# Pair loads, weight chunks, x loads and the last stacks in one chain of issue, x loads from slot 141, all of x split by GpSimd: attention with a softplus MoE on one core

## The chip, the core and the metric

The kernel runs on one core of a Trainium2 chip. The metric is device time in microseconds of one execution. The core has TensorE (PE, with its weight loads as PEld), VectorE (DVE), ScalarE (ACT), GpSimd (POOL) and SyncE (SP); each takes its own list of instructions in order, and sixteen DMA engines move data. SyncE and ScalarE issue the DMAs of this kernel.

## What is computed

Attention over 4 batches, 8 heads, 576 positions and 64 columns a head, with rotary embedding of q and k, and an MoE feed-forward with softplus on its result, all in 32-bit floats:

```
q_rot, k_rot = (rotate(q), rotate(k))
scores = scale * np.matmul(q_rot, k_rot.transpose(0, 1, 3, 2))
scores = scores - np.max(scores, axis=-1, keepdims=True)
attn = np.exp(scores)
attn = attn / (np.sum(attn, axis=-1, keepdims=True) + 1e-09)
return np.matmul(attn, v).astype(np.float32)
...
x = np.ascontiguousarray(attn_out.transpose(0, 2, 1, 3)).reshape(B * S, H * D)
...
h = x @ w_in
g = np.maximum(h, 0.0) + np.log1p(np.exp(-np.abs(h)))
return (g @ w_out).astype(np.float32)
```

x is 2304 x 512, w_in 512 x 2048, w_out 2048 x 512.

## The kernel before, in words

**Precision.** TensorE works on a reduced 32-bit type, so each operand is held as a rounded high part and a low part (the rest), and a product is three matmuls. Splitting an operand is a rounding and a subtraction.

**Attention: slots.** The 32 heads have five blocks of 128 positions each, which gives 160 slots (`NSLOT`); the loop at line 470 runs `NSLOT + LAG + PVD` = 172 times. In slot s, `p1` makes the scores of block s with keys (line 352), and VectorE takes each row's maximum (line 354). Nine slots later (`LAG`), `p2` makes the scores again, transposed and with the maxima taken off (line 389), ScalarE takes the exponential twice (395, 396), and VectorE the low part (403). Three slots on, `pv_mm` multiplies with v (line 421). When a head is through, `evac` copies its sum out and writes it to `xd` and the row sums to `xs` in device memory (lines 429 to 434); after each batch the sums come back as `rc`, `recip` inverts them on VectorE and writes `rd` (line 445).

**The shift row.** In slot 5h GpSimd rounds the five maxima of the last head (`shift1`, tile `shl`), in slot 5h + 1 TensorE transposes them (`shift2`, line 372), ScalarE casts the result (374) and itself issues the small DMA `qs<-shr` that puts it into two rows of q (`shift3`, line 378). `p2` reads it three slots later.

**Loads.** q and k come by pairs of heads: `load_pair` reads two raw tiles of 576 KB (line 287), `rope_steps` turns them, mostly on GpSimd (line 300) one step a slot, and `stack(h)` copies a head's parts with four DMAs into `qs` and `ks` (lines 331 to 334). A pair's first stack is emitted at slot 10p - 4 for use at slot 10p, the second at 10p for use at 10p + 5. All these DMAs are issued by SyncE.

**Weights.** Each w chunk is 128 x 512 in 64 bits, 512 KB (line 105), and is turned into high and low 32-bit parts by `conv_w` on ScalarE and VectorE, one step per call of a hook. f = 0 is converted at the start; `late` holds the others, begun at slot 138 (`WP`). The chunks of f = 1 have tiles of their own (`wr`), the others share three buffers (`wraw`).

**x.** Its first two batches are brought back while attention still runs: `load_xb` reads for each of eight chunks (two batches, four column blocks) the rows of `xd` (288 KB) and twice the inverse sums from `rd`, spread over 64 partitions (144 KB each). `split_xb` multiplies, rounds (both GpSimd) and subtracts. The subtractions of the second batch's first two chunks are VectorE's (`low_xb`, line 189, slots 161 and 163). `tail(s)`, called at the end of each slot, asks for one load a slot from slot 110 (`XL`) and for one step of a split, sometimes two, from slot 146 (`XS`).

**MoE.** 96 units of 384 rows by 128 columns of h: `emit_h` (line 200, tile hp) and two units later `emit_o` (line 236, tiles oa and ob). The first unit reads x of batch 0 alone, the second also batch 1. The first two are placed in the last slots of attention.

**What sets the order.** Instructions that go through `pin` keep the order in which the program emits them. Others (`free`, or none) are placed by a scheduler on their engine's list, sometimes far ahead of where they were emitted. Each DMA signals one of eight completion counters, taken in turn in the scheduled order, SyncE's and ScalarE's together, and a DMA is issued only when the one before it on the same counter has landed.

## Time and profile before

| | us |
|---|---|
| median of three timed runs | 765.46 (762.35 to 766.77) |
| the profiled execution | 767.87 |
| its span | 766.0 |
| TensorE busy, of the span | 723.5 (94%) |
| VectorE busy | 501.5 (65%) |
| ScalarE busy | 383.7 (50%) |
| GpSimd busy | 307.9 (40%) |

Attention takes the first 357 us or so, the MoE the rest. The timeline of an engine lists its instructions by start, with the length, the source line, what is written from what, and in brackets the idle time ahead with what ended it. A DMA's line (SPq, ACTq) is the time of its issue alone: the data lands later. The row of the maxima on VectorE (line 354) stands once in each slot, so that its starts show the pace.

### The profile page before, as it was taken

How to read it: one execution, taken by the hardware profiler on the slowest of the kernel's cores; microseconds unless marked ns; L12 is line 12 of the kernel's file. 1: busy time of each engine (PE TensorE's matmuls, PEld its weight loads, DVE VectorE, ACT ScalarE, POOL GpSimd, SP SyncE). 2: the span in 40 equal slices, each digit the busy share in tenths (PEclk: the TensorE clock that was granted, in tenths of full speed). 3: DMA queues.
4: the chain of work that ended last, by engine and by line, in shares of the span. 5: the costliest groups of instructions: out<-in, count | busy, mean ns of one | idle time of the engine just before them, and what ended most of it. 6: DMA issues, size and time to landing. Idle time of an engine off the chain costs nothing.

```text
span 766.0 us, 11808 instructions
## 1 busy us (share of the span) xinstructions
PE 723.5 (94%) x4288; PEld 674.9 (88%) x4288; DVE 501.5 (65%) x790; ACT 383.7 (50%) x718; POOL 307.9 (40%) x370
## 2 busy tenths in 40 slices
PE   5579999979998999998999999999999999999997
PEld 5469999978998998997889999998999989899996
DVE  7668888857786787886788888864453444444343
ACT  2157777656775776776566556532222222222221
POOL 6249999958887888891000000083040000000000
PEclk9579999999999999999999999999999999999999
DMA  8967888887877789510233333353010001001001
GB/s 261 261 146 193 210 213 213 219 217 203 213 197 204 207 229 213 133 26 9 92 110 110 112 110 111 97 159 110 1 62 1 1 1 42 1 1 42 0 1 42
DMA packets 46507, 91.41 MB, mean 119 GB/s; under 512 B 6800, under 2 KB 15312, under 8 KB 46448
## 3 DMA queue, kind: packets, MB, share of 16 engines
q1 hardware_dynamic: 43472, 85.77, 41.4%
q10 hardware_dynamic: 2976, 4.88, 1.7%
q8 instruction: 34, 0.56, 0.3%
q14 instruction: 25, 0.20, 0.1%
HBM read 51.00 MB, written 9.58 MB: 79 GB/s over the span
## 4 chain that ended last, share of the span: by engine, by line
PE 60%; DVE 3%; ACT 1%; issue 1%; DMA 1%; POOL 0%; DVEq 0%; ACTq 0%; POOLq 0%; SPq 0%
PE hp L200 25%; PE oa L236 12%; PE ob L236 12%; PE pv L421 4%; PE sp L389 3%; PE sp L352 3%; DVE wc L132 1%; DVE wc L129 1%; DMA ks<-raw 1%; DVE e L210 0%; DVE m L215 0%; DVE wl L137 0%; DVE wc L125 0%; ACT e L212 0%; DVE g L220 0%
## 5 line engine op out<-in xcount | busy, mean ns | idle before, releaser
L200 PE MATMUL hp<-x,wh 128*128 128x384 f32 x768 | 196.3, 336 | 0.0
L354 DVE TENSOR_REDUCE mx<-sp 128x1 f32<-128x576 f32 x160 | 121.0, 756 | 74.8 <-PE sp L352 51.7
L200 PEld LDWEIGHTS hp<-x,wh 128*128 128x128 f32 x768 | 140.7, 188 | 8.6 <-ACT wh L135 0.5
L212 ACT ACTIVATE e<-e 128x384 f32<-128x384 f32 x96 | 50.4, 525 | 186.8 <-DVE e L210 182.1
L352 PE MATMUL sp<-ks,qs 128*128 128x288 f32 x640 | 119.1, 311 | 23.2 <-DMA ks<-raw 17.5
L395 ACT ACTIVATE ph<-sp 128x576 fp32r<-128x576 f32 x160 | 103.8, 649 | 57.3 <-PE sp L389 57.1
L200 PE MATMUL hp<-x,wl 128*128 128x384 f32 x384 | 129.6, 337 | 0.6 <-DVE wl L137 0.5
L352 PEld LDWEIGHTS sp<-ks,qs 128*128 128x128 f32 x640 | 97.2, 197 | 28.8 <-issue 19.3
L389 PE MATMUL sp<-qs,ks 128*128 128x288 f32 x640 | 115.0, 302 | 6.0 <-DMA qs<-shr 4.9
L421 PE MATMUL pv<-ph,vs 128*64 128x288 f32 (+1 forms) x640 | 112.6, 299 | 4.4 <-DVE xt L429 3.4
L396 ACT ACTIVATE sp<-sp 128x576 f32<-128x576 f32 x160 | 102.8, 643 | 0.0
L389 PEld LDWEIGHTS sp<-qs,ks 128*128 128x128 f32 x640 | 94.7, 192 | 8.2 <-DMA qs<-shr 5.4
L210 DVE TENSOR_SCALAR e<-hp 128x384 int32<-128x384 int32 x96 | 53.3, 555 | 73.8 <-PE hp L200 73.4
L403 DVE TENSOR_TENSOR pl<-sp,ph 128x576 fp32r<-128x576 f32 x128 | 96.6, 755 | 6.5 <-ACT sp L396 5.1
L236 PE MATMUL oa<-wh,g 128*128 128x512 f32 x288 | 97.7, 393 | 0.0
L236 PE MATMUL ob<-wh,g 128*128 128x512 f32 x288 | 97.3, 393 | 0.0
L421 PEld LDWEIGHTS pv<-ph,vs 128*64 128x64 f32 (+1 forms) x640 | 88.2, 164 | 5.2 <-ACT ph L395 4.8
L300 POOL TENSOR_TENSOR raw<-raw,tab 128x576 f32<-128x576 f32 x58 | 82.5, 1442 | 8.8 <-DMA raw<-qk 8.8
L220 DVE TENSOR_TENSOR g<-m,g 128x384 fp32r<-128x384 f32 x96 | 56.1, 584 | 44.7 <-ACT g L217 44.7
L215 DVE SCALAR_TENSOR_TENSOR m<-hp,e 128x384 f32<-128x384 f32 x96 | 53.5, 557 | 48.6 <-ACT e L212 48.5
L300 POOL TENSOR_TENSOR raw<-raw 128x576 f32<-128x576 f32 (+1 forms) x56 | 80.8, 1443 | 5.2 <-ACT raw L294 3.0
L217 ACT CAST g<-m 128x384 fp32r<-128x384 f32 x96 | 49.1, 512 | 60.0 <-DVE m L215 57.8
(73 smaller groups left out, 875.8 us busy)
## 6 DMA issues: line engine op xcount, KB each, us to landing
raw<-qk SPq DMA_DIRECT2D x32, 576.0 KB
wraw<-w SPq DMA_DIRECT2D x30, 512.0 KB
ks<-raw SPq DMA_DIRECT2D x32, 320.0 KB
qs<-raw SPq DMA_DIRECT2D x32, 288.0 KB
ks<-raw SPq DMA_DIRECT2D x32, 160.0 KB
vf<-v SPq DMA_DIRECT2D x32, 160.0 KB
qs<-raw SPq DMA_DIRECT2D x32, 144.0 KB
xd<-xt SPq DMA_DIRECT2D x32, 144.0 KB
```

The lines of the kernel that those rows point to most:

```text
L200: pin(nc.tensor.matmul(out=hp, lhsT=a[f][:, c * 128:(c + 1) * 128], rhs=piece(j, c)[:, b, :], start=(i == 0), stop=(i == 11),))
L215: pin(nc.vector.scalar_tensor_tensor(out=m, in0=hp, scalar=0.0, in1=e, op0=ALU.max, op1=ALU.add))
L220: pin(nc.vector.tensor_tensor(out=g[:, 1, :], in0=m, in1=g[:, 0, :].bitcast(F32), op=ALU.subtract))
L236: pin(nc.tensor.matmul(out=po, lhsT=g[:, s, t * 128:(t + 1) * 128], rhs=b[f][:, 512:1024], start=(first and i == 0), stop=(last and i == 2),))
L300: pin((nc.vector if e == "V" else nc.gpsimd).tensor_tensor(out=out, in0=in0, in1=in1, op=op))
L352: pin(nc.tensor.matmul(out=sp[:, j, :HS], lhsT=q[:, i, cq], rhs=k[:, 0, ck], start=(i == 0), stop=(i == 1)))
L354: pin(nc.vector.tensor_reduce(out=mx_t[h][:, c:c + 1], in_=sp[:, :, :HS], axis=AX.XY, op=ALU.max, negate=True))
L389: pin(nc.tensor.matmul(out=sp[:, i, :HS], lhsT=k[:, j, ck], rhs=q[:, j, hs], start=(j == 0), stop=(j == 1)))
L395: pin(nc.scalar.activation(out=ph, in_=sp, func=AF.Exp, scale=D ** -0.5))
L396: pin(nc.scalar.activation(out=sp, in_=sp, func=AF.Exp, scale=D ** -0.5))
L403: pin(nc.vector.tensor_tensor(out=pl, in0=sp[:, :, :HS], in1=ph.bitcast(F32), op=ALU.subtract))
L421: pin(nc.tensor.matmul(out=pv[rows, i, :HS], lhsT=lhs, rhs=rhs[:, i, :], start=(c == 0 and j == 0), stop=(c == 4 and j == len(terms) - 1)))
```

## The change

`chain` makes each DMA that goes through it follow the one that went through before, on SyncE's list. Through it go the weight chunks from f = 1 on, the pair loads from the third pair on, the x loads, and the stacks of the last four heads. `XL` goes from 110 to 141, with two x loads a slot after slot 150. All three steps of each split are GpSimd's; `low_xb` and its two places are gone, and the buffer for the products has two tiles instead of four.

```diff
-XL = 110
+XL = 141
...
+    order = []
+
+    def chain(ins):
+        if order:
+            tc.add_manual_dep(ins.ins, order[-1].ins.name,
+                              mybir.DependencyInfo(mybir.DependencyClass.NoSync, mybir.DependencyReason.DATA))
+        order[:] = [ins]
+        return ins
...
-            (pin if n + f < 2 else free)(nc.sync.dma_start(out=raw.bitcast(w.dtype), in_=w[f, :, i * m:(i + 1) * m]))
+            (pin if f == 0 else chain)(nc.sync.dma_start(out=raw.bitcast(w.dtype), in_=w[f, :, i * m:(i + 1) * m]))
...
-        yield nc.sync.dma_start(out=t[:, 0, :], in_=xd[b, c * 128:(c + 1) * 128, :])
+        yield chain(nc.sync.dma_start(out=t[:, 0, :], in_=xd[b, c * 128:(c + 1) * 128, :]))
...
-            yield nc.sync.dma_start(out=t[i * D:(i + 1) * D, 1, :], in_=src)
+            yield chain(nc.sync.dma_start(out=t[i * D:(i + 1) * D, 1, :], in_=src))
...
-        if e is not None:
-            yield pin(e.tensor_tensor(out=t[:, 1, :], in0=x, in1=t[:, 0, :].bitcast(F32), op=ALU.subtract))
...
+        yield pin(nc.gpsimd.tensor_tensor(out=t[:, 1, :], in0=x, in1=t[:, 0, :].bitcast(F32), op=ALU.subtract))
...
-    def low_xb(b, c):
-        t = half_x(b, c)
-        pin(nc.vector.tensor_tensor(out=t[:, 1, :], in0=xraw[b, c], in1=t[:, 0, :].bitcast(F32), op=ALU.subtract))
...
-                (pin if p < 2 else free)(nc.sync.dma_start(out=r[:, :, :S].bitcast(F32), in_=qk[p, i]))
+                (pin if p < 2 else chain)(nc.sync.dma_start(out=r[:, :, :S].bitcast(F32), in_=qk[p, i]))
...
+            keep = chain if h >= 28 else free
+            keep(nc.sync.dma_start(out=q[64:128, 0, :S], in_=qhl[o, 0, :S]))
...
-        mp["xm"] = pool(es, "xm", 4, "right")
+        mp["xm"] = pool(es, "xm", 2, "right")
...
-                next(loads, None)
+                for _ in range(2 if s > NSLOT - 10 else 1):
+                    next(loads, None)
...
-            if s in lows:
-                low_xb(1, lows[s])
...
-        lows = {NSLOT + 1: 0, NSLOT + 3: 1}
-        splits = (x for i in range(8) for x in split_xb(*divmod(i, 4), None if 4 <= i < 6 else nc.gpsimd))
+        splits = (x for i in range(8) for x in split_xb(*divmod(i, 4)))
```

The lists of TensorE and ScalarE are the same in both kernels; VectorE's lacks the two subtractions, and GpSimd's has them. SyncE's differs above all at three places. In the names, qs_120 to qs_123 and ks_116 to ks_119 are the four stack buffers (head modulo 4), x_72 to x_75 the four column blocks of x.

SyncE in the first slots, before: the pair loads (raw with the tile's number), the weight chunks (wraw) and the stacks of heads 2 and 3 (buffers 2 and 3 of qs and ks).

```order
L331 DMA qs2_122<-raw_205 64x576
L332 DMA qs2_122<-raw_205 64x2x576
L331 DMA qs3_123<-raw_205 64x576
L332 DMA qs3_123<-raw_205 64x2x576
L287 DMA raw_350<-qk 128x2x576
L105 DMA wraw_4660<-w 128x512
L287 DMA raw_462<-qk 128x2x576
L333 DMA ks2_118<-raw_251 64x2x640
L333 DMA ks3_119<-raw_251 64x2x640
L334 DMA ks2_118<-raw_251 64x640
L334 DMA ks3_119<-raw_251 64x640
L105 DMA wraw_4665<-w 128x512
```

And now:

```order
L334 DMA qs2_122<-raw_205 64x576
L335 DMA qs2_122<-raw_205 64x2x576
L289 DMA raw_350<-qk 128x2x576
L334 DMA qs3_123<-raw_205 64x576
L335 DMA qs3_123<-raw_205 64x2x576
L336 DMA ks2_118<-raw_251 64x2x640
L336 DMA ks3_119<-raw_251 64x2x640
L337 DMA ks2_118<-raw_251 64x640
L337 DMA ks3_119<-raw_251 64x640
L289 DMA raw_462<-qk 128x2x576
L289 DMA raw_575<-qk 128x2x576
L320 DMA vf0_124<-v 128x320
```

The two weight chunks are gone from here; of the pair loads raw_350 moved ahead of head 3's q, and raw_462 from ahead of the four ks loads to behind them.

SyncE around slots 62 to 70, before: rd is the first batch's inverse sums, and the stacks are those of heads 14 and 15.

```order
L332 DMA qs_122<-raw 64x2x576
L445 DMA rd<-rc 128x36
L318 DMA vf_125<-v 128x320
L161 DMA x_72<-rd 64x576 x2
L161 DMA x_73<-rd 64x576 x2
L433 DMA xd<-xt 64x576
L434 DMA xs<-xt 1x576
L333 DMA ks_118<-raw 64x2x640
L334 DMA ks_118<-raw 64x640
L331 DMA qs_123<-raw 64x576
```

And now:

```order
L335 DMA qs_122<-raw 64x2x576
L448 DMA rd<-rc 128x36
L320 DMA vf_125<-v 128x320
L336 DMA ks_118<-raw 64x2x640
L436 DMA xd<-xt 64x576
L437 DMA xs<-xt 1x576
L337 DMA ks_118<-raw 64x640
L334 DMA qs_123<-raw 64x576
```

The loads of x from rd, which stood between vf and the ks loads, are gone. The same holds 40 slots later, for the second batch.

SyncE around slots 130 to 150, before: wr are the chunks of f = 1, raw is half of the last pair, qs_120 and ks_116 are head 28's.

```order
L287 DMA raw<-qk 128x2x576
L105 DMA wr<-w 128x512 x2
L433 DMA xd<-xt 64x576
L434 DMA xs<-xt 1x576
L331 DMA qs_120<-raw 64x576
L332 DMA qs_120<-raw 64x2x576
L318 DMA vf_125<-v 128x320
L438 DMA rc<-xs 128x36
```

And now, where wr and that half pair stand, with the end of head 28's stack (ks_116) and head 29's (qs_121, ks_117):

```order
L337 DMA ks_116<-raw 64x640
L289 DMA raw<-qk 128x2x576
L113 DMA wr<-w 128x512 x2
L334 DMA qs_121<-raw 64x576
L335 DMA qs_121<-raw 64x2x576
L336 DMA ks_117<-raw 64x2x640
L337 DMA ks_117<-raw 64x640
L320 DMA vf_124<-v 128x320
L166 DMA x_72<-xd 128x576
L169 DMA x_72<-rd 64x576
```

The chunks wr moved from ahead of head 28's stack to behind it, and rc no longer stands behind them. Some rows further on head 30's k (ks_118) and head 31's q (qs_123) are reached; there the list was

```order
L333 DMA ks_118<-raw 64x2x640
L433 DMA xd<-xt 64x576
L434 DMA xs<-xt 1x576
L334 DMA ks_118<-raw 64x640
L331 DMA qs_123<-raw 64x576
L332 DMA qs_123<-raw 64x2x576
```

and is now

```order
L336 DMA ks_118<-raw 64x2x640
L436 DMA xd<-xt 64x576
L437 DMA xs<-xt 1x576
L337 DMA ks_118<-raw 64x640
L169 DMA x_73<-rd 64x576
L166 DMA x_74<-xd 128x576
L169 DMA x_74<-rd 64x576 x2
L334 DMA qs_123<-raw 64x576
```

with the second chunk's last x load (x_73) and the third's behind head 30's k. On GpSimd, each of the eight splits now has its subtraction; the two that were VectorE's stand right behind their roundings.

## Rows read from the trace of the kernel before

**Rows 1.** Timeline of VectorE: the maxima of slots 21, 66, 72, 109, 113, 146

```profile
67.62 0.76 DVE L354 TENSOR_REDUCE mx<-sp 128x1 f32<-128x576 f32 x1 [0.23 <-PE sp L352]
...
150.15 0.76 DVE L354 TENSOR_REDUCE mx<-sp 128x1 f32<-128x576 f32 x1 [0.22 <-PE sp L352]
...
167.87 0.76 DVE L354 TENSOR_REDUCE mx<-sp 128x1 f32<-128x576 f32 x1 [0.42 <-PE sp L352]
...
238.88 0.76 DVE L354 TENSOR_REDUCE mx<-sp 128x1 f32<-128x576 f32 x1 [0.30 <-PE sp L352]
...
250.41 0.76 DVE L354 TENSOR_REDUCE mx<-sp 128x1 f32<-128x576 f32 x1 [0.40 <-PE sp L352]
...
314.22 0.76 DVE L354 TENSOR_REDUCE mx<-sp 128x1 f32<-128x576 f32 x1 [0.22 <-PE sp L352]
```

**Rows 2.** Timeline of SyncE, slots 67 to 69

```profile
153.19 2.72 SPq L161 DMA_DIRECT2D x<-rd  x4
...
157.18 0.64 SPq L333 DMA_DIRECT2D ks<-raw  x1
```

**Rows 3.** Timeline of TensorE, slot 70

```profile
161.98 1.25 PE L352 MATMUL sp<-ks,qs 128*128 128x288 f32 x4 [3.18 <-DMA ks<-raw]
```

**Rows 4.** Timeline of ScalarE, slot 66: the cast and its load

```profile
149.56 0.26 ACT L374 CAST shr<-sp 10x128 fp32r<-10x128 f32 x1
...
153.03 0.62 ACTq L378 DMA_DIRECT2D qs<-shr  x1
```

**Rows 5.** Timeline of TensorE from the start to 52 us

```profile
23.13 5.87 PE L352 MATMUL sp<-ks,qs 128*128 128x288 f32 x20 [9.40 <-DMA ks<-raw]
...
42.61 1.09 PE L389 MATMUL sp<-qs,ks 128*128 128x288 f32 x3 [4.67 <-DMA qs<-shr]
...
46.70 0.76 PE L352 MATMUL sp<-ks,qs 128*128 128x288 f32 x4 [1.08 <-DMA ks<-raw]
```

**Rows 6.** Timeline of SyncE from the start to 52 us

```profile
3.36 1.66 SPq L105 DMA_DIRECT2D wraw<-w  x3
...
18.32 1.12 SPq L334 DMA_DIRECT2D ks<-raw  x1
```

**Rows 7.** The page, part 2: what the DMA engines moved, in 40 slices

```profile
GB/s 261 261 146 193 210 213 213 219 217 203 213 197 204 207 229 213 133 26 9 92 110 110 112 110 111 97 159 110 1 62 1 1 1 42 1 1 42 0 1 42
```

**Rows 8.** An x load of the MoE alone: its issue on SyncE, its reader on GpSimd

```profile
486.46 1.11 SPq L172 DMA_DIRECT2D wraw<-rd  x2
...
490.87 1.18 POOL L176 TENSOR_TENSOR wraw<-wraw 128x384 f32<-128x384 f32 x1 [134.39 <-DMA wraw<-rd]
```

**Rows 9.** Timeline of ScalarE, slot 6: issue of the first shift row

```profile
35.61 1.24 ACTq L378 DMA_DIRECT2D qs<-shr  x1
```

**Rows 10.** Timeline of SyncE, slots 132 to 137

```profile
285.53 1.08 SPq L105 DMA_DIRECT2D wr<-w  x2
...
295.57 0.33 SPq L438 DMA_DIRECT2D rc<-xs  x1
```

**Rows 11.** Timeline of GpSimd, slots 147 to 163

```profile
317.18 1.47 POOL L176 TENSOR_TENSOR xm<-x 128x576 f32<-128x576 f32 x1
...
320.85 0.21 POOL L297 TENSOR_SCALAR shl<-mx 128x5 fp32r<-128x5 f32 x1
...
344.52 1.44 POOL L179 TENSOR_TENSOR x<-xm,x 128x576 fp32r<-128x576 f32 x1
```

**Rows 12.** Timeline of SyncE, slot 147: the end of head 30's stack of k

```profile
315.70 0.85 SPq L334 DMA_DIRECT2D ks<-raw  x1
```

**Rows 13.** Timeline of TensorE, slot 151: the shift matmul

```profile
322.55 0.22 PE L372 MATMUL sp<-identr,shl 128*10 128x128 f32 x1
```

**Rows 14.** End of attention: VectorE, and TensorE behind it

```profile
347.06 1.26 DVE L189 TENSOR_TENSOR x<-xm,x 128x576 fp32r<-128x576 f32 x1
...
351.78 0.77 PE L421 MATMUL pv<-ph,vs 128*128 128x288 f32 x4 [3.42 <-DVE xt L429]
```

**Rows 15.** The chain that ended last, in order of time

```profile
359.87 2.10 PE hp L200 x12
```

More of the change, by code (lines that the diff above doesn't have):

```diff
@@ L173, in load_x, with split, split_xb @@
         xraw[j, c] = raw, rc
-    def split(x, raw, rc, t, e):
+    def split(x, raw, rc, t):
         yield pin(nc.gpsimd.tensor_tensor(out=x, in0=raw, in1=rc, op=ALU.mult))
         yield pin(nc.gpsimd.tensor_scalar(out=t[:, 0, :], in0=x, scalar1=1.0, scalar2=0.0, op0=ALU.mult, op1=ALU.add))
-        if e is not None:
-            yield pin(e.tensor_tensor(out=t[:, 1, :], in0=x, in1=t[:, 0, :].bitcast(F32), op=ALU.subtract))
-    def split_xb(b, c, e):
+        yield pin(nc.gpsimd.tensor_tensor(out=t[:, 1, :], in0=x, in1=t[:, 0, :].bitcast(F32), op=ALU.subtract))
+    def split_xb(b, c):
         t = half_x(b, c)
         x = mp["xm"].tile([128, S], F32, tag="xm", name="xm")
-        xraw[b, c] = x
-        return split(x, t[:, 0, :].bitcast(F32), t[:, 1, :].bitcast(F32), t, e)
-    def low_xb(b, c):
-        t = half_x(b, c)
-        pin(nc.vector.tensor_tensor(out=t[:, 1, :], in0=xraw[b, c], in1=t[:, 0, :].bitcast(F32), op=ALU.subtract))
+        return split(x, t[:, 0, :].bitcast(F32), t[:, 1, :].bitcast(F32), t)
     def split_x(j, c):
         raw, rc = xraw.pop((j, c))
-        return split(raw, raw, rc, piece(j, c), nc.gpsimd)
+        return split(raw, raw, rc, piece(j, c))
     def emit_h(j, f):
@@ L330, in stack @@
             qhl, khl = hl_t[p, 0].bitcast(F32), hl_t[p, 1].bitcast(F32)
-            nc.sync.dma_start(out=q[64:128, 0, :S], in_=qhl[o, 0, :S])
-            nc.sync.dma_start(out=q[0:64, :, :S], in_=qhl[o, :, :S])
-            nc.sync.dma_start(out=k[0:64], in_=khl[o, 0:1, :].to_broadcast([64, 2, SP]))
-            nc.sync.dma_start(out=k[64:128, 0, :], in_=khl[o, 1, :])
+            keep = chain if h >= 28 else free
+            keep(nc.sync.dma_start(out=q[64:128, 0, :S], in_=qhl[o, 0, :S]))
+            keep(nc.sync.dma_start(out=q[0:64, :, :S], in_=qhl[o, :, :S]))
+            keep(nc.sync.dma_start(out=k[0:64], in_=khl[o, 0:1, :].to_broadcast([64, 2, SP])))
+            keep(nc.sync.dma_start(out=k[64:128, 0, :], in_=khl[o, 1, :]))
         mx_t, sh_t, ps2, p_t, pv_t, rc_t = {}, {}, {}, {}, {}, {}
```

## Prediction

> **What bounds the kernel now.** I read the profile in four steps: the chain of waits and the window table for the stages, the timeline of VectorE for the pace, the timelines of SyncE and TensorE where the pace breaks, and the timeline of GpSimd where the change puts work. From about 390 us the chain is TensorE alone, matmul behind matmul, to the end; the change touches nothing there. So the gain or loss lies in the attention stage before it.
>
> The stage runs in slots, and VectorE's row maximum (line 354) stands once in each, so its starts are a ruler. From slot 21 to slot 66 they go from 67.62 to 150.15 us: 82.53 us in 45 slots, 1.834 us a slot, with no break [rows 1]. From slot 66 to 146 the ruler goes to 314.22: 164.07 us, where 80 slots at that pace are 146.7. **17.4 us are lost between 150 and 314 us.** They are not spread: slots 66 to 72 take 17.72 instead of 11.0 (6.7 lost), 72 to 109 take 71.01 instead of 67.9 (3.1), 109 to 113 take 11.53 instead of 7.3 (4.2), 113 to 146 take 63.81 instead of 60.5 (3.3) [rows 1].
>
> The first and largest shows what ends last. At 153.19 SyncE issues four loads x<-rd (2.72 us); only after them, at 157.18, the ks load of head 14 [rows 2], and TensorE waits 3.18 us for it, until 161.98 [rows 3]. The x loads of slots 110 and later had been moved this far ahead, and SyncE takes its list in order. There is a second path: each DMA in the built program signals one of eight counters in turn and is issued only when the eighth before it has landed. The extra loads push the shift row's load, issued by ScalarE, onto a counter whose last user is late: it stands at 153.03, where the cast that it needs began at 149.56 and takes a quarter of a microsecond [rows 4], and ScalarE's exponentials stand behind it. The 4.2 us at slot 110 are the same four loads for the next batch, and the 3.1 us after slot 72 are mostly GpSimd's rope work, late by what it lost at 68 to 70.
>
> The head of the kernel is the other place. TensorE starts slot 0 at 23.13 after 9.40 us of waiting for ks, waits 4.67 us at 42.61 for the first shift row, and 1.08 us at 46.70 for the third head's ks [rows 5].
>
> **The change, part by part.**
>
> *x loads from slot 141.* All 24 leave the stretch from 73 to 250 us. No order of SyncE between slots 16 and 130 holds anything new. Of the 17.4 us I leave 1.0 for the two reciprocals on VectorE (slots 102 and 142), work that stays. Ends: the whole 16.5, or only the two clusters that directly have x<-rd in front of ks, 6.7 + 4.2 = 10.9. I take 16.4, since the rest follows the clusters on GpSimd's queue or comes from the weight chunks (next). **-16.4.**
>
> *Weight chunks kept late.* Before, five raw chunks of 512 KB are read in the first 40 us, where two are needed: one too many in the issue at 3.36 [rows 6], and the two that the order shows further on. The DMA engines move 261 GB/s there [rows 7], so each is 2.0 us of transfer. The order now has two, and puts a raw load (576 KB, 2.2 us) behind ks of head 2 that stood ahead of it. First wait: ks is issued at 18.32 for 1.12 us [rows 6] and lands at 23.13. A load into SBUF that stood alone landed 3.3 us behind its issue (487.57 to 490.87) [rows 8], which would be 22.7; so between 0.4 and 2.0 us, I take 0.9. Second wait: the shift row is issued 35.61 to 36.85 [rows 9] and lands at 42.6, 5.7 us later; with the queue short of two chunks and one raw load, 3.3 us, so 39.3 with the 0.9: 3.3 earlier. The third wait, 1.08, then falls away, as ks has 3 us less ahead of it. 0.9 + 2.5 + 1.1 = 4.5; ends 0.4 (only the first floor) and 6.5 (all transfers). **-4.5.**
>
> *Weight chunks of f = 1 at slot 138.* Before, they are issued at 285.53, and SyncE's next wait on their counter ends at 295.57 [rows 10], ten microseconds later, with ks of slot 140 behind it; that is most of the 3.3 us lost from 113 to 146, counted above. Now they stand behind the last pair load and ahead of head 29's stack, in slot 138. With the old loss at slot 140 taken out, slot 138 begins near 297 in the old time (314.22 less 8 slots, less 2.4 lost between), and the issue follows at some 298. About 0.7 MB less is queued ahead of them, 2.7 us at the 261 GB/s, so the second lands near 305 to 307. The eighth DMA after it, on the same counter, is head 27's shift row, which ScalarE wants at slot 141, near 302 (322.55 [rows 13] less ten slots, less the 2.4). ScalarE waits some 4 us with all exponentials behind it. Finished score tiles carry TensorE on for less than a slot, so it loses between 4 - 1.83 = 2.2 and 4; I take 2.8; ends 0 (it lands in 4 us) and 5 (it takes its ten again, and the clock falls as it does after the 3.18 us at slot 70). **+2.8.**
>
> *The splits on GpSimd.* Its queue is full from 313 us: the eight chunks stand back to back with the shift rounding and v's low part. Two more subtractions of 1.44 us [rows 11] make 2.9 us, but they stand behind the last shift rounding but one, and the last chunk, whose subtraction began at 344.52 [rows 11], is read only by the second MoE unit, whose matmuls begin at 359.87 [rows 15]: that cover hides them. Without it the 2.9 would come on top. What is not hidden is the wait for the loads. The second chunk's last x load now stands behind ks of head 30, whose issue is 315.70 to 316.55 [rows 12]; it goes out to 317.1 and lands by the lone load's 3.3 us [rows 8] at 320.4, where GpSimd wants it at 317.18. From there to the shift rounding it has 3.67 us of work (320.85) [rows 11], ending 0.5 later, and TensorE takes that result at 322.55 [rows 13], 1.2 us of room. So 3.2 - 1.2 = 2.0 us at slot 151. As GpSimd has no idle time to catch up, the next two roundings (slots 156, 161) come late by another 0.5 together. Ends 0 and 4. **+2.5.**
>
> *VectorE freed of two subtractions.* At 347.06 one of 1.26 us stands in the row of work that ends with the copy for which TensorE waits 3.42 us, to 351.78 [rows 14]. It goes, and nothing else in that row waits. **-1.2**; ends 0 (another engine is then last) and 2, if part of the slow clock behind the wait goes too. The other has idle time behind it: nothing.
>
> *Order kept among pair loads and the last stacks.* SyncE loses no time by it: 0, covered by the 4 slots between a stack and its use.
>
> **Sum:** -16.4 - 4.5 + 2.8 + 2.5 - 1.2 = -16.8 us. The profiled execution took 767.87 (span 766.0 and 1.87 around it): 751.1. It lies 2.4 above the median of the three timed runs, 765.46; from that the sum gives 748.7. The waits that go are also what varies between runs, so I take a little over the middle: **750**.
>
> A page of the Trainium skill speaks against the change: DMA: Bandwidth & Descriptors, in its rules for kernel authors, says to issue a DMA early and wait for it late, so that its fixed cost is covered by compute. By that rule the old placement was right and the new one exposes a wait for each chunk. The trace of before agrees for the loads themselves, GpSimd never waited for x at 313 to 347 us, and disagrees for the kernel, since the early issue held up other loads. What the rule would make of the time is the third rival below.
>
> **The rivals.**
>
> 1. *The follow-on losses aren't the x loads'.* GpSimd is close to full with rope work, and slots 80, 90, 100, 120 and 140 may be tight by themselves. For it: each lies at a pair's first slot. Against: slots 20 to 60 have the same order and lose nothing. Then 3.1 + 3.3 less 0.9 = 5.5 us stay: 755.5.
>
> 2. *Neither new wait shows.* The chunks land in 4 us and the x loads in time. For it: the queue is lighter at both places. Then 750 - 5.3: 745.
>
> 3. *Late loads starve GpSimd; slower.* All eight chunks wait as the second does. Place: GpSimd's queue from slot 146, where the shift roundings of three heads and v's low parts stand behind the splits, and the MoE's second unit behind the last chunk. Price: eight waits of w, with 1.2 us of room. The other terms are a gain of 19.3, so from w = 3.0 us (8 x 3.0 - 1.2 = 22.8, past 19.3 by 3.5) it is slower by the bound below; with w = 3.3, as the lone load has it, 25.2 - 19.3: 774. Against: from the third chunk on each load is issued a chunk ahead, and GpSimd takes 3.7 us for a chunk.
>
> **How the numbers follow.** Forecast 0.60, with its own range of 746.5 to 754; rival 1 0.17; rival 2 0.16; rival 3 0.04; a mix of rival 1 with the poor ends of the new waits, near 763, 0.03. A measurement of this kernel can tell about 0.5%, 3.8 us, from no change. Faster by more: 0.92; within: 0.04; slower: 0.04. The range takes in rivals 1 and 2 in their middle: 743 to 757.5.
>
> **What would show it.** Right: the ruler keeps 1.834 us a slot from 66 to 138 but for the reciprocals; no x<-rd stands between a raw load and ks before slot 141; the first shift row's wait at TensorE is under 2.5 us. ScalarE's shift row load of slot 141 stands over 2 us behind its cast; GpSimd waits for an x load once, before slot 151; the copy at the end of attention comes about 1.2 us sooner behind its matmuls. Wrong: losses at slots 80, 100 or 120 as before (rival 1), GpSimd waiting at most chunks (rival 3), or a new wait between 16 and 66. From the first MoE unit to the end the two kernels should differ by under 1 us.

## The result, and the profile after

| | before | after |
|---|---|---|
| median, us | 766.12 (762.35 to 770.02, 4 runs) | 755.39 (753.01 to 756.95, 4 runs) |
| the profiled execution, us | 767.87 | 753.01 |
| its span, us | 766.0 | 751.2 |

The ratio is 0.985 (95% interval 0.982 to 0.989): faster by 1.5%, 10.7 us, where 15.5 were forecast. The median lies in the range on record, 743 to 757.5, but outside the forecast's own, 746.5 to 754, and next to the number of the first rival, 755.5. The two traces differ by 14.8 us of span, more than the medians do: the profiled execution of before lies 1.8 us above its median, that of after is the fastest of its four.

The ruler of row maxima, VectorE's line 357 now, answers to [rows 1]. These are the starts at slots 21, 66, 72, 109, 113, 138, 142, 145, 150 and 157 in the timeline of VectorE (start, length, line, in brackets the idle time ahead):

```profile
63.07 0.76 DVE L357 TENSOR_REDUCE mx<-sp 128x1 f32<-128x576 f32 x1 [0.23 <-PE sp L355]
...
145.57 0.76 DVE L357 TENSOR_REDUCE mx<-sp 128x1 f32<-128x576 f32 x1 [0.23 <-PE sp L355]
...
156.59 0.76 DVE L357 TENSOR_REDUCE mx<-sp 128x1 f32<-128x576 f32 x1 [0.33 <-PE sp L355]
...
224.47 0.76 DVE L357 TENSOR_REDUCE mx<-sp 128x1 f32<-128x576 f32 x1 [0.30 <-PE sp L355]
...
231.78 0.76 DVE L357 TENSOR_REDUCE mx<-sp 128x1 f32<-128x576 f32 x1 [0.39 <-PE sp L355]
...
277.61 0.76 DVE L357 TENSOR_REDUCE mx<-sp 128x1 f32<-128x576 f32 x1 [0.39 <-PE sp L355]
...
284.93 0.76 DVE L357 TENSOR_REDUCE mx<-sp 128x1 f32<-128x576 f32 x1 [0.33 <-PE sp L355]
...
296.09 0.76 DVE L357 TENSOR_REDUCE mx<-sp 128x1 f32<-128x576 f32 x1 [1.86 <-PE sp L355]
...
305.27 0.76 DVE L357 TENSOR_REDUCE mx<-sp 128x1 f32<-128x576 f32 x1 [0.41 <-issue]
...
319.90 0.76 DVE L357 TENSOR_REDUCE mx<-sp 128x1 f32<-128x576 f32 x1 [0.32 <-PE sp L355]
```

From 66 to 138 there is 132.04 us for 72 slots, 1.834 each, the pace of slots 21 to 66; slots 72, 109 and 113 come 11.02, 67.88 and 7.31 us behind one another, where before had lost 6.7, 3.1 and 4.2. What break there is lies in the three intervals from 142 to 145: 11.16 us, where the same three take 5.65 in the heads before (slots 122 to 125). In the trace of before, the starts at slots 138, 142 and 145 are these; it loses 2.0 us from 138 to 142, and only 0.46 from 142 to 145:

```profile
297.15 0.76 DVE L354 TENSOR_REDUCE mx<-sp 128x1 f32<-128x576 f32 x1 [0.41 <-PE sp L352]
...
306.47 0.76 DVE L354 TENSOR_REDUCE mx<-sp 128x1 f32<-128x576 f32 x1 [0.31 <-PE sp L352]
...
312.58 0.76 DVE L354 TENSOR_REDUCE mx<-sp 128x1 f32<-128x576 f32 x1 [0.65 <-PE sp L352]
```

The chain of waits of after (start, length, what) says what that break is:

```profile
277.81 8.72 DMA wr<-w
286.53 0.02 issue
286.55 4.86 DMA qs<-shr
```

The second wr chunk is issued at 277.81 and lands 8.72 us later; 0.02 us behind that, ScalarE issues head 27's shift row, which has nothing to do with the chunk but its counter: seven DMAs stand between the two, so that the chunk is the eighth before the row. ScalarE's timeline (ACTq is a DMA's issue) has the cast of that row at 282.48, so it and the exponentials were held; TensorE's has the wait for the row's landing behind it:

```profile
282.48 0.26 ACT L377 CAST shr<-sp 10x128 fp32r<-10x128 f32 x1
...
286.55 0.62 ACTq L381 DMA_DIRECT2D qs<-shr  x1
287.22 0.65 ACT L398 ACTIVATE ph<-sp 128x576 fp32r<-128x576 f32 x1 [3.41 <-PE sp L355]
...
289.25 0.40 PE L392 MATMUL sp<-qs,ks 128*128 128x288 f32 x1 [1.71 <-DVE pl L406]
291.45 0.66 PE L392 MATMUL sp<-qs,ks 128*128 128x288 f32 x3 [1.80 <-DMA qs<-shr]
```

(The third line names TensorE as the releaser; but the issue stands ahead of that exponential in ScalarE's order, and it is the issue that the chain follows back to wr.)

The second new wait is GpSimd's, for the second x chunk (the profile names x<-xd; the last load of the chunk is the x<-rd that SyncE issues at 298.86), and the shift rounding behind it makes TensorE wait at slots 151 and 156. Timelines of SyncE, GpSimd and TensorE:

```profile
298.33 0.48 SPq L337 DMA_DIRECT2D ks<-raw  x1
298.86 0.60 SPq L169 DMA_DIRECT2D x<-rd  x1
...
302.49 1.47 POOL L184 TENSOR_TENSOR xm<-x 128x576 f32<-128x576 f32 x1 [2.98 <-DMA x<-xd]
...
306.70 0.23 PE L375 MATMUL sp<-identr,shl 128*10 128x128 f32 x1 [0.47 <-POOL shl L302]
317.20 0.23 PE L375 MATMUL sp<-identr,shl 128*10 128x128 f32 x1 [1.17 <-POOL shl L302]
```

The start and the end, beside [rows 5] and [rows 14], in TensorE's timeline: the first ks wait, the first shift row, and the copy at the end of attention.

```profile
22.01 4.44 PE L355 MATMUL sp<-ks,qs 128*128 128x288 f32 x16 [9.45 <-DMA ks<-raw]
...
38.27 1.09 PE L392 MATMUL sp<-qs,ks 128*128 128x288 f32 x3 [1.40 <-DMA qs<-shr]
...
336.62 1.04 PE L424 MATMUL pv<-ph,vs 128*128 128x288 f32 x4 [2.81 <-DVE xt L432]
```

### The profile page after: what moved, and what is told of

The parts are those of the page before. It is cut to its first block, busy times and chain, and to the rows that moved or that the text cites. A ratio compares the mean times of both kernels' runs of the same rounds, so it can differ in the third digit from the quotient of the medians.

```text
span 751.2 us, 11818 instructions
## 1 busy us (share of the span) xinstructions
PE 718.7 (96%) x4288; PEld 672.6 (90%) x4288; DVE 498.0 (66%) x788; ACT 383.4 (51%) x718; POOL 310.3 (41%) x372
## 4 chain that ended last, share of the span: by engine, by line
PE 82%; DVE 6%; DMA 5%; ACT 3%; POOL 2%; issue 1%; SPq 1%; ACTq 0%; DVEq 0%; POOLq 0%
PE hp L202 25%; PE pv L424 13%; PE oa L238 12%; PE ob L238 12%; PE sp L355 10%; PE sp L392 10%; DVE raw L302 2%; DMA wr<-w 1%; DMA qs<-shr 1%; DVE wc L140 1%; DMA tab<-cs 1%; DVE wc L137 1%; DMA ks<-raw 1%; DMA wraw<-w 1%; DVE e L212 0%
## 5 line engine op out<-in xcount | busy, mean ns | idle before, releaser
L355 PE MATMUL sp<-ks,qs 128*128 128x288 f32 x640 | 117.3, 308 | 13.0 <-DMA ks<-raw 9.4
```

The source lines that it names most:

```text
L355: pin(nc.tensor.matmul(out=sp[:, j, :HS], lhsT=q[:, i, cq], rhs=k[:, 0, ck], start=(i == 0), stop=(i == 1)))
```

## The experiments

All runs in one table: the median, its ratio to the median of before on the same chip, and from each kernel's one trace the length of a stretch between two starts of the ruler. Each column thus tells one place from another, which the median doesn't. "End" is from slot 159's start to the end of the span.

| kernel | median, us | ratio (95%) | slots 0 to 11 | 66 to 138 | 138 to 142 | 142 to 145 | 150 to 157 | 157 to 159 | end |
|---|---|---|---|---|---|---|---|---|---|
| before | 766 to 767 | 1 | 25.04 | 147.00 | 9.32 | 6.11 | 12.66 | 3.71 | 427.9 |
| after | 755.39 | 0.985 (0.982 to 0.989) | 21.63 | 132.04 | 7.32 | 11.16 | 14.63 | 3.70 | 427.6 |
| x_free | 767.75 | 1.002 (1.000 to 1.005) | 21.92 | 146.70 | 7.31 | 10.05 | 13.53 | 3.71 | 429.5 |
| w_free | 758.34 | 0.989 (0.986 to 0.993) | 25.55 | 132.03 | 7.32 | 11.40 | 14.64 | 3.70 | 427.7 |
| wr_slot140 | 751.67 | 0.982 (0.978 to 0.986) | 21.25 | 132.06 | 7.30 | 9.92 | 13.93 | 3.71 | 427.3 |
| wr_slot158 | 752.67 | 0.983 (0.980 to 0.986) | 20.96 | 132.12 | 7.32 | 7.50 | 16.35 | 3.71 | 428.6 |
| raw_first | 749.31 | 0.977 (0.974 to 0.981) | 21.85 | 132.02 | 7.32 | 5.67 | 15.50 | 3.70 | 429.5 |
| wr158_x138 | 750.28 | 0.979 (0.976 to 0.982) | 21.18 | 132.13 | 7.34 | 7.27 | 12.66 | 4.67 | 427.8 |
| wr158_x120 | 758.99 | 0.990 (0.987 to 0.993) | 21.47 | 138.89 | 7.31 | 8.71 | 14.40 | 3.70 | 429.1 |
| together | 751.04 | 0.980 (0.977 to 0.983) | 21.24 | 132.03 | 7.32 | 5.67 | 12.67 | 7.12 | 428.8 |
| wr_apart | 750.22 | 0.979 (0.976 to 0.981) | 22.64 | 132.10 | 7.30 | 5.67 | 12.67 | 5.62 | 429.1 |
| x_sparse | 752.55 | 0.981 (0.978 to 0.985) | 21.21 | 133.82 | 7.34 | 5.66 | 13.78 | 4.68 | 429.2 |
| low_on_dve | 748.37 | 0.977 (0.973 to 0.981) | 22.10 | 132.03 | 7.32 | 5.67 | 12.67 | 5.84 | 427.0 |
| row_chained | 750.69 | 0.982 (0.978 to 0.985) | 21.87 | 132.03 | 7.31 | 5.68 | 15.79 | 3.69 | 426.4 |

**The x loads alone (x_free).**

```diff
-XL = 141
+XL = 110
...
-        yield chain(nc.sync.dma_start(out=t[:, 0, :], in_=xd[b, c * 128:(c + 1) * 128, :]))
+        yield free(nc.sync.dma_start(out=t[:, 0, :], in_=xd[b, c * 128:(c + 1) * 128, :]))
...
-            yield chain(nc.sync.dma_start(out=t[i * D:(i + 1) * D, 1, :], in_=src))
+            yield free(nc.sync.dma_start(out=t[i * D:(i + 1) * D, 1, :], in_=src))
```

> Of the changed kernel, only the x loads are out of the chain; the number of the slot they are asked for is 110 again, which alone moves nothing: with 141 the built program has the same order. They go to slots 67 to 70 and 110, as before. Theory: 17 us are lost again between slots 66 and 142, and the waits that the late x loads bring are gone (2.0 us at slots 151 and 156), as is part of the 5.1 us at slots 143 to 145, since no x load stands there: 755.4 + 17 - 2 - 1.5 = 769 at most, and with the 3 to 4 us at slots 110 to 140 that the weight chunks may have caused left out, 765. Rival: most of the old losses came with the free weight chunks or pair loads; then it is under 760.

The kernel is as slow as before. Between slots 66 and 138, 14.66 us are back, the clusters at 68 to 71 and 110 to 112 and the follow-on losses at slots 80, 90 and 100 (0.8, 1.0 and 1.0) with them, though the weight chunks stay where the change put them. At slot 120 only 0.2 us of the 0.9 that before loses there came back; what else took that loss away isn't shown. Slots 142 to 145, where no x load stands now, still lose 4.4 us, 1.1 less than in after. It is the chain that does the work: with `XL` at 141 and the loads out of the chain, the built program has the same order on every engine as x_free. In SyncE's timeline the four loads stand ahead of ks again, and in TensorE's the wait:

```profile
150.54 2.64 SPq L169 DMA_DIRECT2D x<-rd  x4
...
154.40 0.64 SPq L336 DMA_DIRECT2D ks<-raw  x1
...
159.12 1.09 PE L355 MATMUL sp<-ks,qs 128*128 128x288 f32 x4 [2.98 <-DMA ks<-raw]
```

**The weight chunks alone (w_free).**

```diff
-            (pin if f == 0 else chain)(nc.sync.dma_start(out=raw.bitcast(w.dtype), in_=w[f, :, i * m:(i + 1) * m]))
+            (pin if n + f < 2 else free)(nc.sync.dma_start(out=raw.bitcast(w.dtype), in_=w[f, :, i * m:(i + 1) * m]))
```

> Of the changed kernel, only the weight chunks are as they were before: free, so that three more of f = 1 and on are read within the first 40 us; the rest of the chain stands. Theory (the prediction's term of 4.5 us, of which the profiles of the variants leave 3.7, since the first matmul of the same program starts anywhere within 1.3 us): slot 11 starts 3.5 to 4 us later than in the changed kernel, nothing else moves, 755.4 + 3.7 = 759.1. Rival: the early chunks only take the place of idle time, as the first waits have other causes (rope work of the first pairs on GpSimd), and the time is within 1 us of 755.4.

The theory holds: 25.55 us from slot 0 to 11, as before has 25.04, and 20.96 to 22.64 in the twelve traces without the early chunks (mean 21.6). That is 3.7 us by the traces (the mean of the two against the mean of the twelve), 2.9 by the medians of w_free and after. All of it lies behind slot 0, whose start differs from trace to trace, with or without the early chunks: 23.3 to 25.1 us. In TensorE's timeline the wait for the first shift row, 1.40 us in after, is back:

```profile
43.34 1.09 PE L392 MATMUL sp<-qs,ks 128*128 128x288 f32 x3 [5.07 <-DMA qs<-shr]
```

**wr elsewhere (wr_slot140, wr_slot158).**

```diff
-WP = 138
+WP = 140
```

> One number is changed: the two weight chunks wr are asked for at slot 140 instead of 138. In SyncE's list they move from ahead of head 29's stack to behind it and its v load, two DMAs ahead of the first x load; the bytes that are moved stay the same. The DMA eight places ahead of the shift row of slot 141 is then a load of q for head 29 instead of the second wr chunk. Theory (shared counter): ScalarE issues that shift row within 0.6 us of its cast, where the changed kernel took 4.07 us from cast to issue (282.48 to 286.55), and the slots 143 to 145 lose under 2 us instead of 5.1; the time is 755.4 less 3 to 4, near 752. Rival (the DMA engines are full there, whoever is held up): the shift row lands as late as before, the three slots lose 3.5 us or more, and the time stays within 1.5 us of 755.4. Under both, the second x chunk's loads now wait for wr, and head 30's stack behind them.

By the place, the rival was nearer: the three slots still lose 4.3 us. The DMA eight places ahead of the row is a q load now, issued at 278.72, and ScalarE still holds the row for 1.92 us:

```profile
283.39 0.26 ACT L377 CAST shr<-sp 10x128 fp32r<-10x128 f32 x1
...
285.31 0.62 ACTq L381 DMA_DIRECT2D qs<-shr  x1
```

It then takes 5.70 us to land (the chain; 4.86 in after), with wr issued right ahead of it, at 283.51. Taking wr off the counter saves 1.24 of the 5.5 us, and the rest stays with the same bytes in the queue. By the time, the theory's number came: the median fell by 3.7, to 751.67; but the span of the trace is only 1.4 us shorter than that of after, so the traces don't explain it.

```diff
-WP = 138
+WP = 158
```

> The chunks wr are asked for at slot 158, behind the last x load, so that neither their counters nor their bytes are anywhere near slots 138 to 146. Theory: the 5.1 us lost at slots 143 to 145 all go, and nothing else changes: the chunk is first read by ScalarE at slot 162 or so; 750.3. The wait of GpSimd for the second x chunk stays, since its last load still stands behind head 30's k: slots 151 and 156 lose 2.0 us as before. Rival (raw tile, two stacks and the x loads are too much there by themselves): 2 to 3 us of the 5.1 stay, 753.

3.66 of the 5.5 us go, 1.85 stay. Its chain at that place has a q load, 6.60 us from issue to landing, and the row again nearly five:

```profile
278.66 6.60 DMA qs<-raw
285.26 0.02 issue
285.28 4.75 DMA qs<-shr
```

So neither theory was right alone, though the rival was near (it had 2 to 3 us stay where 1.85 do, and 753 where 752.67 came). And 1.7 of the 3.66 us are handed back at slots 150 to 157: slot 145 comes 3.66 us sooner behind slot 142, the last load of the second x chunk only 2.1.

**The last raw tile (raw_first).**

```diff
+                if s % 10 in (2, 6) and s // 10 + 2 < NP:
+                    load_pair(s // 10 + 2, (s % 10 // 4,))
                 if s % 10 == 6 and h // 2 + 1 < NP:
                     stack(h + 1)
-                if s % 10 in (2, 6) and s // 10 + 2 < NP:
-                    load_pair(s // 10 + 2, (s % 10 // 4,))
```

> As wr_slot158, and in slot 136 the last pair load is emitted ahead of head 28's stack instead of behind it. In the chain that puts the raw tile twelve places earlier on SyncE's list, where the kernel before had it; nothing else of the chain changes its order but the first x loads, which move up by two or three places. Theory: keeping the last stacks in the chain was not free, as the prediction had it; the raw tile (576 KB) came late and fell together with the stacks of heads 28 and 29, which is what still holds the shift row of slot 141 in wr_slot158 (1.9 us from cast to issue, then over 4 us to land). Here slots 143 to 145 lose under 0.5 us, 1.5 us less than in wr_slot158: 751.2. Rival: the x loads are what fills the DMA engines there; then the three slots still lose 1.2 us or more, and the time is that of wr_slot158, 752.7.

5.67 us: nothing is lost at slots 142 to 145. The row goes out right behind its cast:

```profile
284.19 0.26 ACT L377 CAST shr<-sp 10x128 fp32r<-10x128 f32 x1
284.35 0.64 ACT L398 ACTIVATE ph<-sp 128x576 fp32r<-128x576 f32 x1
284.48 0.62 ACTq L381 DMA_DIRECT2D qs<-shr  x1
```

The rest of the 5.5 us is thus the raw tile, which the chain put behind head 28's stack (the edit also moves the first x loads up by two or three places). The shares of wr and of the tile hold for this order of taking them away; the tile first with wr still at slot 138 was not run. The price of wr at slot 158 shows at the end: the two wr chunks and three more are issued from 318.48 on, ahead of head 31's shift row, which needs 7.51 us to land (the chain), and TensorE waits 3.75 of them:

```profile
324.06 7.51 DMA qs<-shr
...
331.61 1.20 PE L392 MATMUL sp<-qs,ks 128*128 128x288 f32 x7 [3.75 <-DMA qs<-shr]
```

**Earlier x loads (wr158_x138, wr158_x120, x_sparse).**

```diff
-WP = 138
+WP = 158
...
-XL = 141
+XL = 138
```

> wr at slot 158 as in wr_slot158, and x loads from slot 138 instead of 141: the second x chunk is complete ahead of head 30's stack. Theory: GpSimd doesn't wait for x ahead of slot 151, and slots 151 and 156 lose less by 1.5 to 2.0 us: 748.5. Rival: the three slots are no matter, as GpSimd's queue is full anyway and the shift roundings come late by its own work: within 0.7 us of wr_slot158. A second rival: three x loads among the raw tile and the stacks make TensorE wait for ks at slot 145 or 150, and it is slower than wr_slot158 by 1 us or more.

Slots 150 to 157 take 12.66 us, as before: GpSimd doesn't wait and the 1.97 us of after are gone, so that term was theirs. A new 0.97 comes at slot 158, where two x loads are asked for in each slot: ScalarE holds the shift row of slot 156 from 312.50 to 315.01, and the eighth DMA before it is an x load, 5.93 us from issue to landing. The median is 750.28, 1.8 above the theory's.

```diff
-WP = 138
+WP = 158
...
-XL = 141
+XL = 120
```

> wr at slot 158, x loads from slot 120, one a slot, kept in the chain, so that they lie between the loads of heads 25 to 30, as early loads did in the kernel before, but never more than one or two ahead of a ks load. Theory: what cost the kernel before its 17 us was where the x loads stood in line and which counter that gave, not that they were early; here they cost nothing, GpSimd never waits for x, and the time is that of wr158_x138, 748.5 (747 to 750). Rival (the transfers themselves are the price: DMA engines are at 0.79 there before any x load): stacks come late at slots 125 to 145, TensorE waits for ks again, 752 to 756.

Slower, as the rival had it, and by more (752 to 756 were its bounds), but TensorE doesn't wait for ks: 6.8 us go in one place, slots 128 to 130. ScalarE holds the shift row of slot 126 for 7.2 us, and the profile names a load qs<-raw as what ended it. That is the DMA eight places ahead of the row, and four x loads and a raw tile were issued in the 7 us before it:

```profile
254.91 0.26 ACT L377 CAST shr<-sp 10x128 fp32r<-10x128 f32 x1
...
262.11 0.64 ACTq L381 DMA_DIRECT2D qs<-shr  x1
262.80 0.65 ACT L398 ACTIVATE ph<-sp 128x576 fp32r<-128x576 f32 x1 [6.56 <-DMA qs<-raw]
```

```diff
-            if s >= XL:
-                for _ in range(2 if s > NSLOT - 10 else 1):
-                    next(loads, None)
+            if s >= XL and (s > 140 or s % 4 == 0):
+                next(loads, None)
```

(with raw_first's edit, XL 92, WP 158)

> The last raw tile first, wr at slot 158, and the x loads much earlier but thin: the first batch's twelve one every four slots from 92 on, the second batch's from 141, one a slot. Against wr158_x120, where one a slot from 120 cost 6.8 us at slots 128 to 130, this tells earliness from crowding. Theory: an x load costs when it stands among the DMAs that a shift row's counter or a stack has to wait for while the queue is deep; thin ones find room, since the DMA engines are busy 0.79 of the time there: under 0.5 us lost between slots 92 and 140, and 747 to 748.5 in all. Rival: each x load put among the stacks shifts which DMA stands eight ahead of the shift rows, and some land on a raw tile or a k load: 2 us or more lost between 92 and 140, 750 or above.

Near the rival: 1.8 us are lost from 66 to 138, not 6.8 and not under 0.5, and the median, 752.55, lies in its range. Thin loads cost less, not nothing.

**All together, and what it ran into (together, wr_apart, low_on_dve, row_chained).**

```diff
-WP = 138
+WP = 152
...
-XL = 141
+XL = 138
...
-                for _ in range(2 if s > NSLOT - 10 else 1):
-                    next(loads, None)
+                next(loads, None)
```

(with raw_first's edit)

> All that the runs so far point to: the last raw tile ahead of head 28's stack, x loads from slot 138 and one a slot to the end (two a slot from 151 made the shift row of slot 156 wait 2.5 us for its counter in wr158_x138), wr at slot 152. Theory: against wr158_x138 (750.3) the 1.7 us at slots 143 to 145 and the 1.2 us at slot 158 go: 747.4; ScalarE issues each shift row from slot 136 on within 0.6 us of its cast. Rival: wr at slot 152 takes their place and holds the shift row of slot 156, which stands nine DMAs behind it, or the x loads: 749 to 751.

The rival. Up to slot 157 nothing is lost any more, then 3.4 us at once, by the same mechanism: the chain has the load x<-xd that stands behind the two wr chunks, 8.08 us to its landing, and 0.02 behind it the shift row of slot 156, whose cast was at 310.74.

```profile
307.60 8.08 DMA x<-xd
315.68 0.02 issue
315.70 0.62 ACTq L381
```

```diff
-            if s == WP:
-                for x in late:
-                    next(x)
+            if s in (WP, WP + 4):
+                next(late[s > WP])
```

(on together, WP 158)

> As together, but the two wr chunks are taken apart and asked for at slots 158 and 162, behind nearly all x loads, in place of slot 152. In together the DMA eight places ahead of the shift row of slot 156 was an x load that stood right behind the two chunks, ScalarE held that row 4.96 us (310.74 to 315.70), its wait ended with a load x<-xd, and slots 158 and 159 lost 3.4 us. Here it is an x load with only x loads ahead of it. Theory: the row goes out within 0.6 us of its cast, no slot from 66 to 159 loses more than 0.2 us but for the reciprocals, and the time is 751.0 - 3.4 = 747.6. Rival: one x load a slot is itself what holds that row there; then slots 156 to 159 still lose 1 us or more, and it is 749 or above.

The rival again, and smaller: the row is held 2.0 us (312.20 to 314.20) by an x load among x loads, and slots 157 to 159 lose 1.9. The median is 750.22.

```diff
+        lows = {NSLOT + 1: 0, NSLOT + 3: 1}
-        splits = (x for i in range(8) for x in split_xb(*divmod(i, 4)))
+        splits = (x for i in range(8) for x in split_xb(*divmod(i, 4), None if 4 <= i < 6 else nc.gpsimd))
...
+            if s in lows:
+                low_xb(1, lows[s])
```

(on wr_apart; `low_xb` and the four tiles for the products are as in before)

> wr_apart with one part of the change undone: the low parts of the second batch's first two x chunks are subtracted by VectorE again, at slots 161 and 163 (four tiles for the products instead of two). Theory (the prediction's term of 1.2 us): TensorE's wait for the copy at the end of attention is longer by 0.7 to 1.3 us than in wr_apart. Rival (the profiles so far: 3.42 us before, 2.8 to 3.1 in the runs without the two subtractions): ScalarE and TensorE set the copy's start as much as VectorE does, and the wait differs by 0.6 us or less; the time by less than can be told.

Neither: the wait for the copy at the end of attention, here and in wr_apart, is shorter with the two subtractions on VectorE, first low_on_dve, then wr_apart:

```profile
332.09 0.76 PE L430 MATMUL pv<-ph,vs 128*128 128x288 f32 x4 [2.76 <-DVE xt L438]
```

```profile
334.39 1.30 PE L424 MATMUL pv<-ph,vs 128*128 128x288 f32 x4 [3.94 <-DVE xt L432]
```

The waits of the other traces without the subtractions (1.94 in row_chained, 2.81 in after, 0.48 in raw_first) differ by more than the 1.26 us of a subtraction, so that one trace of each can't tell the edit's share. The median of low_on_dve is 1.85 us below that of wr_apart on the same chip, again not the way of the theory; the runs of the two overlap (747.25 to 749.83 and 748.76 to 751.16).

```diff
-            pin(nc.scalar.dma_start(out=qs[h % NST][64:66, 1, :].bitcast(F32).rearrange("p (c q) -> p c q", c=5),
-                                    in_=shr.bitcast(F32)))
+            (chain if h >= 28 else free)(pin(nc.scalar.dma_start(
+                out=qs[h % NST][64:66, 1, :].bitcast(F32).rearrange("p (c q) -> p c q", c=5), in_=shr.bitcast(F32))))
...
-                next(loads, None)
+                for _ in range(2 if s in (144, 149) or s > NSLOT - 4 else 0 if s in (151, 153, 155, 156) else 1):
+                    next(loads, None)
```

(on wr_apart)

> As wr_apart, but the shift rows of the last four heads (slots 146, 151, 156 and 161) go through the chain too, and no x load is asked for in slots 151, 153, 155 and 156 (two at once in slots 144, 149 and from 157). So only three x loads stand between the shift rows of slots 151 and 156 where ten loads and a wr chunk stood, the fourth x chunk of the second batch and the wr chunks stand behind, and the DMA eight ahead of the row of slot 156 is an x load of the chunk before, issued some 9 us earlier. The work of ScalarE keeps its order. Theory (counter): that row goes out within 0.6 us of its cast instead of 2.0, slots 158 and 159 lose under 0.4 us instead of 1.9, and the time is 750.2 - 1.7 = 748.5. Rival (the lateness of the row is that of a full DMA queue, not of the counter): the cast-to-issue time falls, but TensorE waits for the row's landing as long as before, 750.2. A second rival: GpSimd now waits for the last three x chunks, and slot 161 or the second unit of the MoE is late by 1 us or more.

The theory holds at its place and fails as a whole. The row of slot 156 goes out 0.3 us behind its cast and slots 157 to 159 take 3.69, so the counter was what held it. But the loads that were moved ahead now hold the row of slot 151 by 3.7 us, and 3.1 us are lost there, with 0.8 more at slot 150, where TensorE waits for ks:

```profile
303.12 0.26 ACT L377 CAST shr<-sp 10x128 fp32r<-10x128 f32 x1
...
306.80 0.62 ACTq L381 DMA_DIRECT2D qs<-shr  x1
```

All variants but x_free, w_free and wr158_x120 have medians 2.7 to 7.0 us below that of after, whose own four runs lie 3.9 us apart. The first two are raw_first, 6.1 us ahead, and low_on_dve, 7.0; the 0.9 between these is within their spread (748.70 to 751.87 and 747.25 to 749.83).

## Why the prediction was right, and where it was off

The median is in the range, but the number alone would speak for the first rival, 755.5, and not for the forecast, 750. The range was wide enough for both. What speaks for the forecast's reasons are the traces and the variants, not the median: for the profiled execution its sum gave 751.1, and 753.01 came. By its own steps, with the trace of after against that of before; the five sum to the 14.8 us of span:

| step | predicted | measured |
|---|---|---|
| x loads from slot 141 (with what wr had cost at slot 140) | -16.4 | -17.0 |
| early weight chunks | -4.5 | -4.55 in the trace, of which 1.1 is the start of slot 0 |
| wr at slot 138, and the order kept | +2.8 and 0 | +5.05 |
| GpSimd's wait for x | +2.5 | +1.97 |
| VectorE freed, and the rest | -1.2 | -0.3 |

**The x loads** were sized right, and the reason stands: x_free brings 14.66 back. The 2.0 us of slots 138 to 142, which it doesn't bring back, are put down to wr's old place by [rows 10], where SyncE waits ten microseconds ahead of ks; no run has wr alone back there. The first rival, that the follow-on losses have another cause, falls with x_free but for the 0.7 us of slot 120. The 1.0 us left for the reciprocals was not needed: the intervals from 102 to 105 take 6.11 us in before and 5.67 in after, as the same three do at other heads. Rival 2 fell, as both new waits show, and rival 3, as GpSimd waited for x twice and not at eight chunks. (Its 774 is reckoned from the profiled execution, where the forecast starts from the median; from that it would be 771.)

**The early chunks**: the second wait is 3.3 us shorter, where 2.5 were reckoned (4.67 before, 1.40 after), and the third, 1.08, is gone; of both together the stretch from slot 0 to 11 shows 3.4. The first was not right. The 0.9 us for the first ks rest on a wait (9.40 before, 9.45 after) that didn't change, and the start of slot 0 differs by as much between traces with the same order there. 3.4 to 3.7 us remain of the 4.5.

**wr at slot 138** is where the mechanism was right and the size was not. The chunk landed in 8.72 us (7 to 9 were reckoned), and the row was held 4.07 us (some 4 reckoned). The step that failed is the one from there to the loss: "it loses between 4 - 1.83 = 2.2 and 4". It lets the row work from its issue on. In after the row needs another 4.86 us to land, with the DMA engines' busy share at 0.98 from 277 to 297 us (0.80 from 130 to 250). TensorE, which has waited 1.71 us, waits 1.80 more, and four matmuls behind it take up to 1.16 us instead of 0.70: the granted clock is 0.66 in the mean from 291.4 to 295.0, where it was 1.00 up to 291.4. The prediction had such a fall of the clock in the upper end of this term, 5, and not in its 2.8.

**"Order kept among pair loads and the last stacks ... 0"** is the second failed step. It asks whether SyncE would lose time by the order, not what the order brings together. The raw tile, twelve places later, is 1.83 us of the loss (wr_slot158 against raw_first).

**GpSimd's wait** came as reckoned: the load by 3.44 us in a chain like it (wr_slot158), a wait of 2.98 against the 3.2. It was spread otherwise over slots 151 and 156 (0.63 and 1.33 instead of 2.0 and 0.25), and GpSimd waited a second time, 1.26 us ahead of slot 156, where one wait was expected (the profile puts it down to TensorE; in raw_first, with 0.95 us at the same place, to a load x<-rd). The rule of issuing early, of the Trainium skill (DMA: Bandwidth & Descriptors, Rules for kernel authors), is borne out by this one term and against the x loads of slots 66 to 138; wr158_x120 and x_sparse show that earlier is worse again.

**VectorE freed**: the step took the copy's wait to end with VectorE's row of work. In after that wait is 0.6 us shorter than in before, and low_on_dve gives no sign that the subtraction is why. No run shows this term, and a term of its size couldn't be told from the spread of that wait.

So 14.8 instead of 16.8 by the traces, where the errors of the steps partly cancel. That the medians give only 10.7 is not explained by any step: the profiled executions lie 1.8 above and 2.4 below their medians, and the early start of slot 0, 1.1 us, may be part of that. Where the rest lies can't be seen, as the other executions have no trace. That the prediction's choice of 750, a little above its sum from the median, lay on the right side is luck: nothing here shows its reason, that the waits that go are what varies between runs.

## What to carry to other kernels

When DMAs of two engines share a few completion counters in turn, look for each small urgent DMA at the one that holds its counter, and at how many bytes stand ahead of that one; a chunk that nobody needs soon can stop an engine that has no use for it yet. Moving such loads often moves a part of the loss with them, as wr_slot158, together and row_chained show, and no place tried here is shown to be free; raw_first gained by undoing a pile-up. Keeping an order costs what it brings together, so price the bytes in one stretch of the list, not only the instructions.

## What was not expected of the hardware

A shift row has 5 KB, yet at slot 141 it took 4.75 us from issue to landing in wr_slot158, 4.86 in after, 5.70 in wr_slot140 and 6.56 in x_free, and 7.51 at slot 161 of raw_first, with five chunks of 512 KB issued just before. In x_free:

```profile
293.27 6.68 DMA wr<-w
299.95 0.02 issue
299.97 6.56 DMA qs<-shr
```

The row is issued by ScalarE, on a queue of its own (q10 in the page; SyncE's is q1). The Trainium skill (DMA: Bandwidth & Descriptors, Queues, rings and completion order) says that each DMA engine takes turns, packet by packet, between the queues that have work. One would expect from it that the row passes SyncE's backlog. The packets in the trace of after show where the time goes. These are the queues (packets, MB, share of the engines) from the row's issue at 286.55 to 290.33, and then from 290.33 to 291.45:

```profile
q1 hardware_dynamic: 487, 0.89, 106.4%
```

```profile
q1 hardware_dynamic: 157, 0.28, 95.4%
q10 hardware_dynamic: 12, 0.01, 2.0%
```

None of the row's packets starts in the first 3.8 us; then all twelve do. At slot 161 of before, with no other packet under way, they start 1.25 us behind the issue. So the row is late ahead of its first packet. Whether it waits there for a turn or isn't in its queue yet, the trace doesn't tell; it neither bears the rule out nor speaks against it, and the cause stays open.
